# Lag tables of a state-space convolution stored entry by entry, with two products of a complex step in one VectorE instruction

## The chip, the core and the metric

The kernel runs on one core of one Trainium2 chip: TensorE (PE in the profile) multiplies matrices, VectorE (DVE) and ScalarE (ACT) do elementwise work and empty the accumulators (PSUM), SyncE (SP) issues all DMAs, GpSimd (POOL) does a few memsets. The metric is the device time of one execution in microseconds (us), the median of several runs.

## The reference, cut to what matters

Two branches over x (2048 tokens, 512 channels) are mixed by a gate per token.

```python
g = sigmoid((x * gate_w).sum(-1, keepdims=True))
a = attention(x)          # 32 heads of 16, 4 segments of 512 tokens, causal softmax + a memory of earlier segments, then @ wo
dt = exp(log_dt)[:, None]
P = exp((dt * A)[:, :, None] * l)                  # A complex, (512 channels, 128 states); l = 0..2047 rounded to bf16
K = einsum('dn,dnl,dn->dl', C, P, dt * B).real     # convolution kernel, one value per channel and lag
b = irfft(rfft(x) * rfft(K)) + x * Dskip           # causal convolution along the tokens
return g * a + (1 - g) * b
```

Only 640 different lags are left when l is rounded to bf16. The kernel writes each lag as a sum of two exponents, one from a list F_EXP (20 entries) and one from G_EXP (32 entries: 0, 8, ... 248). With z = exp(dt A), K at lag f + g is the real part of a sum over the 128 states of (z to the f) times (C dt B z to the g).

## The kernel before, in words

**Stages.** A preparation computes z and its squares z^2, z^4, ... (ten powers for each half of the channels; the program calls them pw, 512 bf16 values per table of 128 channels: real, real, imaginary twice with a minus sign on one copy, so that a complex product becomes two elementwise products and one sum). Then three things share the engines. Attention works by segment and head group: projections, scores in four banks of PSUM, one exponential of 128x2048 on ScalarE per score tile (line 1068, 80 of them), products with V, norms. The first level of a Fourier transform of x goes to DRAM and back. And `tables(c)` builds, for each quarter c of the channels, the two **lag tables** F (20 entries) and G (32 entries) with the 128 states on the partitions. When all four tables are through, the convolution runs: 32 steps u, each with one product K (five matmuls of 512 columns, line 1273), an elementwise product Y (line 1281), a product V. Sixteen final blocks (line 1307) add the attention's output projection, the inverse transform and the skip term, and scale by the gate. The first matmuls of a final block load weights whose columns lie 16 values (32 bytes) apart.

**A lag table.** Five copies put the first entries in place (tag tabc). Then `cmul` makes n new entries from n old ones by multiplying them with one power: line 1165 multiplies by the first 256 values of the power into the new entries, line 1168 multiplies by the other 256 into a scratch tile t2, line 1172 adds t2 with its halves swapped. Each is one VectorE instruction of 256 n values per partition. A table has 13 such steps: n = 1 three times, n = 2 four times, n = 4 three times, n = 8 three times. That is 39 instructions for a table, 156 in all.

**The layout before.** Channels are stored in pairs: for the real part and then the imaginary part, 64 channel pairs; within a pair all entries, each as two neighbouring channel values. So one new entry (n = 1) is 128 runs of two values (4 bytes), 80 bytes apart in F and 128 bytes in G. The **lag products** (line 1213) take for one channel the 32 entries of G as weights (128x32) and the 20 entries of F as moving columns, each entry 4 bytes behind the one before. Per table there are 256 of these pairs of weight load and matmul, in 8 groups of 32 (four channels at a time in four column groups of the array); the result goes through one copy per half (line 1215) and four small DMAs to a tile KTT, which every K product reads.

**What sets the order.** Nothing is scheduled at run time. ORDER is a list made beforehand: it names every operation by number in one sequence, the engine of each copy that may go to either (a = ACT, v or no letter = DVE), and the buffer. Each engine runs its operations in the order of the list and waits on semaphores for the operations it needs.

Of the kernel before, what the change touches and what calls it, by code (L numbers as in the profile page):

```python
# [98 lines left out]
class Sched:  # L99
# [45 lines left out]
    def ap(self, T, off=0, dims=None, p0=0, np_=128, n=None, dt=None, pstep=1):  # L145
        dt = dt or T.dt
        T = T.tile
        esz = 4 if dt == F32 else 2
        if T.isp:
            h = self.ps32 if dt == F32 else self.ps16  # L150
            base = T.slot * 2048 // esz
        else:
            h = self.sb32 if dt == F32 else self.sb16
# [5 lines left out]
        return bass.AP(v.tensor, v.offset + p0 * st + base + off, [[pstep * st, np_]] + [list(d) for d in dims])  # L159

# [208 lines left out]
0/0 10/0 9/1 23/0/0 24v 15/0 29/0 31/0 38/1 32/2 30/3 33/4 13/2 14/3 27/4/1 39/5 37/6 34 35 40/7 54/0 57/1 6/0 36  # L369
193/0 4/0 41 42 43 44/8 48/0 45/9 46/10 12/4 47 49/11 53/0 50/12 17/0 61/1 59/0 62v/0 51/13 58a/0 60 71/1 52 65/2 11/5  # L370
55/2 56v 73/2 7/0 74v/1 25/3/2 26a 200/5/0/0 201a 250/0/1/1 72 83/3 1247/1 1250/6/0 214/1/0/0 28v 215 75 86v/2 205/0
85/3 173/4 3/0 21/0 66/5 16/0 253/2/0 84 95/0 178/6 20/0 18/0 97/7 98a/3 1226/0 176/1 1/0 251a 96 107/2 63 181/3
1248/7 254a 109/0 1249a 22/0 99 110v/4 202 67 189/0 108 377/0 208/3 190 177/0 252 203/0/1 204a 174/0 196/2 255/0/1/1
191 1251a 119/2 240/0/0 87 79/1 241 120/2 111 209a 122v/5 100 121 123 394/3/1 179/1 256 175 257 133/3 182 88 242
996v/0 395a 131/2 124 132 219/0/1 220 221 146a/6 77/0 998v/0 134v/7 192/0 1003/0 135 143/3 206/3 76 995v 212/0 1002
228/0/2 217 64 994v 1004 145/7 997v 213a 112 1008 1009/1 144 216 1252 229 230 78 1010 210/0 211a 1000/0 223/0/3 224
197/0 198/0 1015/1 147 158v/8 1014 999 136 1016 157/4 207a 235/1 1229/2/1 159 89/2 1001 1012/1 225 222/0 1017 155/3
1230a 1237/3/0 1018/0 1238a 799/0 266/0/1 267 293/2/2/2 226 156 1005 227 231 199/0 268 1011 91/0 1013 236/0/3 167a/9
148 1026 294a 237 588/0 589/3 590 160 168 1020 238 1021/1 232/0 169 90 233 334/2/0/0 335a 1019 1227/3 1228a 234/0
262/0/2 263 1231 264 337/2/2 338a 1022 800/3 239 243 244 1239/0 1240a 245/1 1241 101/0 1029 271/0/3 272 1024/0 273 801  # L380
# [81 lines left out]
def fft_consts():  # L462
# [35 lines left out]
    return W1, M2, N2, G2  # L498


F_EXP = [1, 3, 5, 7, 2, 4, 6, 8, 258, 260, 262, 264, 516, 520, 772, 776, 1032, 1288, 1544, 1800]
G_EXP = [8 * j for j in range(32)]


# [925 lines left out]
```

## Time and profile before

| what | value |
|---|---|
| median of 3 runs | 305.98 us (304.79 to 306.7) |
| the profiled execution | 305.48 us, of which its span is 303.3 us |
| mean granted TensorE clock | 0.958 |
| PE, DVE, ACT busy | 263.6, 264.7, 263.1 us |

The span is the time from the first to the last instruction; some 2.2 us of the execution lie around it. A line number in a row of the profile is a line of the program; most matmuls carry the helper's line 686, and copies out of PSUM the lines 226 (on ACT) and 227 (on DVE). Two successive instructions of DVE or ACT overlap a little, so the time that an instruction takes of its engine is the distance to the next start (the pitch here), not its own length.

### The profile page before, as it was taken

To read this page: it belongs to the slowest core of one execution; us is meant where nothing else is said; L and a number is where in the kernel's file an instruction comes from. 1 tells how busy PE (TensorE), PEld (TensorE's weight loads), DVE (VectorE), ACT (ScalarE), POOL (GpSimd) and SP (SyncE) were. 2 spreads that over 40 slices of the span, in tenths; PEclk is the share of its full clock that TensorE was granted. 3 is DMA by queue.
4 is the path that set the end of the run, shared out by engine and by line. 5 is a ranking of instruction groups with operands and counts; after the bars stand their busy time and mean duration, and the time that the engine had idled before them with its cause. 6 is when DMAs were issued, how large, how long until landed. Compare 5 with 4: busy or idle time off the path is not lost.

```text
span 303.3 us, 9592 instructions
## 1 busy us (share of the span) xinstructions
PE 263.6 (87%) x4078; PEld 150.3 (50%) x4078; DVE 264.7 (87%) x639; ACT 263.1 (87%) x315; POOL 3.2 (1%) x9
## 2 busy tenths in 40 slices
PE   2697698799687888788889999999999999999992
PEld 1442355665344544565446555555545455546551
DVE  2999999999999998999998799999999869957171
ACT  3999999999999899999989998998899999985321
POOL 2000000000000000000000000000000000000000
PEclk9999899789996879999979999999999999999999
DMA  6983722216012331630500516766767756741033
GB/s 150 276 216 90 130 73 71 71 28 185 19 52 53 111 98 40 197 93 17 134 2 18 145 59 197 208 197 180 210 169 212 200 157 187 208 143 46 11 152 126
DMA packets 45002, 37.37 MB, mean 123 GB/s; under 512 B 21408, under 2 KB 40864, under 8 KB 44960
## 3 DMA queue, kind: packets, MB, share of 16 engines
q1 hardware_dynamic: 44960, 36.77, 43.0%
q8 instruction: 32, 0.52, 0.7%
q14 instruction: 10, 0.08, 0.1%
HBM read 18.54 MB, written 6.29 MB: 82 GB/s over the span
## 4 chain that ended last, share of the span: by engine, by line
PE 52%; DVE 22%; ACT 17%; DMA 4%; issue 2%; SPq 1%; ACTq 0%
PE psum L686 51%; ACT sb L1068 9%; DVE sb L1168 5%; DVE sb L1172 5%; ACT sb L226 4%; DVE sb L1165 4%; DMA sb<-in_A_wo_dram 2%; DMA sb<-in_B_log_dt_dram 1%; ACT sb L794 1%; SPq L222 1%; DMA sb<-sb 1%; ACT sb L948 1%; ACT sb L802 1%; DVE sb L227 1%; DVE sb L1122 1%
## 5 line engine op out<-in xcount | busy, mean ns | idle before, releaser
L686 PE MATMUL psum<-sb 128*32 128x20 bf16 (+11 forms) x3990 | 256.4, 232 | 26.0 <-ACT sb L1068 15.0
L686 PEld LDWEIGHTS psum<-sb 128*128 128x128 bf16 (+3 forms) x3990 | 143.6, 97 | 136.6 <-ACT sb L1068 30.0
L1068 ACT ACTIVATE sb<-psum 128x2048 bf16<-128x2048 f32 x80 | 151.4, 1893 | 7.4 <-PE psum L686 6.4
L226 ACT ACTIVATE sb<-psum 128x512 bf16<-128x512 f32 (+2 forms) x152 | 86.1, 615 | 6.8 <-PE psum L686 6.2
L227 DVE CAST sb<-psum 128x512 bf16<-128x512 f32 (+1 forms) x50 | 32.9, 674 | 6.1 <-PE psum L686 5.6
L1165 DVE TENSOR_TENSOR sb<-sb 128x512 bf16<-128x512 bf16 (+3 forms) x52 | 33.9, 660 | 0.1
L1172 DVE TENSOR_TENSOR sb<-sb 128x512 bf16<-128x512 bf16 (+3 forms) x52 | 33.8, 662 | 0.2
L1168 DVE TENSOR_TENSOR sb<-sb 128x512 bf16<-128x512 bf16 (+3 forms) x52 | 33.7, 658 | 0.1
L1080 DVE TENSOR_TENSOR sb<-sb 128x1024 bf16<-128x1024 bf16 (+1 forms) x40 | 22.5, 575 | 1.1 <-ACT sb L1068 0.8
L1281 DVE TENSOR_TENSOR sb<-sb 128x1024 bf16<-128x1024 bf16 x32 | 21.8, 685 | 1.2 <-ACT sb L226 0.8
L229 ACT ACTIVATE sb<-psum,sb 128x512 bf16<-128x512 f32 (+1 forms) x8 | 5.4, 688 | 13.4 <-PE psum L686 13.4
L1043 DVE TENSOR_TENSOR sb<-psum,sb 128x256 bf16<-128x256 f32 x32 | 13.2, 419 | 0.4
L230 DVE TENSOR_SCALAR sb<-psum,sb 128x512 f32<-128x512 f32 (+1 forms) x8 | 6.0, 748 | 8.4 <-PE psum L686 8.3
L794 ACT ACTIVATE sb<-sb 128x512 f32<-128x512 f32 x18 | 11.7, 667 | 0.0
L1040 DVE RECIPROCAL sb<-psum 128x16 f32<-128x16 f32 x32 | 8.0, 250 | 1.7 <-PE psum L686 1.7
L742 PE MATMUL psum<-sb 128*128 128x128 bf16 x24 | 3.1, 309 | 6.8 <-DMA sb<-in_B_A_re_dram 4.1
L1122 DVE TENSOR_TENSOR sb<-psum,sb 128x512 bf16<-128x512 f32 x12 | 8.3, 688 | 0.3
L1338 DVE SCALAR_TENSOR_TENSOR sb<-psum,sb 128x512 bf16<-128x512 f32 x8 | 5.5, 746 | 3.0 <-PE psum L686 3.0
L948 ACT ACTIVATE sb<-psum 128x512 bf16<-128x512 bf16 x12 | 7.7, 638 | 0.5 <-PE psum L945 0.4
L795 DVE TENSOR_TENSOR sb<-sb 128x256 f32<-128x256 f32 x18 | 7.4, 416 | 0.5 <-ACT sb L794 0.5
L999 ACT ACTIVATE sb<-sb 128x512 bf16<-128x512 bf16 x12 | 7.6, 633 | 0.0
L796 DVE SCALAR_TENSOR_TENSOR sb<-sb 128x256 f32<-128x256 f32 x18 | 7.5, 417 | 0.0
(67 smaller groups left out, 105.1 us busy)
## 6 DMA issues: line engine op xcount, KB each, us to landing
sb<-sb SPq DMA_DIRECT2D x64, 128.0 KB, 3.1
sb<-c_DN SPq DMA_DIRECT2D x32, 224.0 KB, 3.1
scr_Z<-sb SPq DMA_DIRECT2D x16, 256.0 KB, 2.4
sb<-scr_Z SPq DMA_DIRECT2D x16, 256.0 KB, 3.5
sb<-in_A_x_dram SPq DMA_DIRECT2D x5, 512.0 KB, 4.6
out_dram<-sb SPq DMA_DIRECT2D x8, 256.0 KB, 2.0
sb<-sb SPq DMA_DIRECT2D x20, 64.0 KB, 2.2
sb<-c_M SPq DMA_DIRECT2D x4, 256.0 KB, 4.4
```

Source lines behind the costliest of these rows:

```text
L226: fa = lambda e: e.activation(dst(), src(), ACT.Copy)
L227: fd = lambda e: e.tensor_copy(dst(), src())
L686: mm = lambda e, o_, l, r_, st, sp, **kw: e.matmul(o_, lhsT=l, rhs=r_, start=st, stop=sp, skip_group_check=True, **kw)
L794: op("ACT", ("As", 512), lambda e, sq=sq, Z=Z: e.activation(ap(sq, n=512), ap(Z, n=512), ACT.Square), r=[Z], w=[sq], key=PW[h] + PWS * k)
L1043: op("DVE", ("V1", 256), lambda e: e.tensor_tensor(ap(o1, gi * 16, [[128, 4], [32, 4], [1, 16]]), ap(T, dims=[[68, 4], [17, 4], [1, 16]]), ...
L1068: o = op("ACT", ("Ax", 2048), lambda e, P=P, pT=pT: e.activation(ap(pT, n=2048), ap(P, n=2048), ACT.Exp, scale=0.25), r=[P], w=[pT])
L1080: op("DVE", ("V2", 128 * nb), lambda e, pT=pT, dims=dims: e.tensor_tensor(ap(pT, dims=dims + [[1, 128]]), ap(pT, dims=dims + [[1, 128]]), ...
L1122: op("DVE", ("V1", 512), lambda e: e.tensor_tensor(ap(o2, 0, [[128, 4], [16, 8], [1, 16]]), ap(P2, 0, [[256, 4], [17, 8], [1, 16]]), ap(R2 ...
L1165: op("DVE", ("V2", 256 * n), lambda e: e.tensor_tensor(run(tile, ne, dst, 1), run(tile, ne, src, sstep), ap(pw, cl * 512, [[2, 128], [0, n ...
L1168: op("DVE", ("V2", 256 * n), lambda e: e.tensor_tensor(run(t2, n, 0, 1), run(tile, ne, src, sstep), ap(pw, cl * 512 + 256, [[2, 128], [0, ...
L1172: op("DVE", ("V2", 256 * n), lambda e: e.tensor_tensor(D_(), D_(), ap(t2, n * 128, [[-n * 128, 2], [2 * n, 64], [1, 2 * n]]), ALU.add), r= ...
L1281: op("DVE", ("V2", 1024), lambda e, Y=Y, XAB=XAB, K3=K3, xo=xo: e.tensor_tensor(ap(Y, dims=[[512, 2], [1, 512]]), ap(XAB, xo, [[512, 2], [ ...
```

## The change

Layout: a table now holds its entries one behind the other, each as 256 neighbouring values (128 real, 128 imaginary). One new entry is one run of 256 values. For the lag products the columns of one channel now lie 256 values (512 bytes) apart, both as weights and as moving columns.

Steps: lines 1165 and 1168 become one instruction of 512 n values: its outer dimension of two goes over the two halves of the power, reads the same old entries twice (step 0) and writes first into the table and then into t2, at the distance between the two tiles. The sum stays one instruction of 256 n values. F_EXP is reordered so that a table needs 12 steps: n = 1 once (G), n = 2 five times, n = 4 three times, n = 8 three times. That is 24 instructions for a table, 96 in all. No DMA is added or removed (207 before and after).

```diff
-F_EXP = [1, 3, 5, 7, 2, 4, 6, 8, 258, 260, 262, 264, 516, 520, 772, 776, 1032, 1288, 1544, 1800]
+F_EXP = [1, 3, 6, 8, 2, 4, 262, 264, 258, 260, 5, 7, 520, 516, 776, 772, 1032, 1288, 1544, 1800]
...
+    def adr(self, T):
+        return (T.pool.addr + T.slot * T.pool.size) // 2
...
-            op("DVE", ("V2", 256 * n), lambda e: e.tensor_tensor(run(tile, ne, dst, 1), run(tile, ne, src, sstep),
-                                                                 ap(pw, cl * 512, [[2, 128], [0, n], [1, 2]]), ALU.mult),
-               r=rd + [pw], w=wr + [tile])
-            op("DVE", ("V2", 256 * n), lambda e: e.tensor_tensor(run(t2, n, 0, 1), run(tile, ne, src, sstep),
-                                                                 ap(pw, cl * 512 + 256, [[2, 128], [0, n], [1, 2]]), ALU.mult),
-               r=rd + [pw], w=[t2])
-            D_ = lambda: ap(tile, 2 * dst, [[ne * 128, 2], [2 * ne, 64], [1, 2 * n]])
+            both = lambda: S.adr(t2) - S.adr(tile) - 256 * dst
+            op("DVE", ("V2", 512 * n), lambda e: e.tensor_tensor(
+                ap(tile, 256 * dst, [[both(), 2], [256, n], [1, 256]]), ap(tile, 256 * src, [[0, 2], [256 * sstep, n], [1, 256]]),
+                ap(pw, cl * 512, [[256, 2], [0, n], [1, 256]]), ALU.mult), r=rd + [pw], w=wr + [tile, t2])
+            D_ = lambda: ap(tile, 256 * dst, [[256, n], [128, 2], [1, 128]])
             op("DVE", ("V2", 256 * n), lambda e: e.tensor_tensor(
-                D_(), D_(), ap(t2, n * 128, [[-n * 128, 2], [2 * n, 64], [1, 2 * n]]), ALU.add), r=[t2], w=wr)
+                D_(), D_(), ap(t2, 128, [[256, n], [-128, 2], [1, 128]]), ALU.add), r=[t2], w=wr)
...
-        fm(1, 0, 1, 1, 1)
+        fm(1, 0, 5, 2, 1)
...
-        fm(2, 0, 1, 2, 2)
+        fm(10, 0, 1, 2, 2)
...
-        fm(6, 4, 1, 1, 2)
...
-        fm(8, 4, 1, 4, 8)
-        fm(12, 5, 2, 4, 9)
+        fm(6, 2, 1, 4, 8)
+        fm(12, 3, 2, 4, 9)
...
-                                i = mm(e, ap(P, sl * NF, n=NF, p0=32 * dq, np_=32), ap(G, (1 - cc) * GPL + (dl // 2) * 2 * NG + dl % 2, [[2, NG]]),
-                                       ap(F, cc * FPL + (dl // 2) * 2 * NF + dl % 2, [[2, NF]]), cc == 0, cc == 1, tile_position=(0, 32 * dq))
+                                i = mm(e, ap(P, sl * NF, n=NF, p0=32 * dq, np_=32), ap(G, (1 - cc) * 128 + dl, [[256, NG]]),
+                                       ap(F, cc * 128 + dl, [[256, NF]]), cc == 0, cc == 1, tile_position=(0, 32 * dq))
```

The ORDER list is replaced as a whole. What it changes can be counted from the two lists. Over the whole program five copies of 512 columns out of PSUM go from ACT to DVE (144 to 139 on ACT, 48 to 53 on DVE), one of 1024 columns goes the same way, two casts of powers (lines 802 and 803) too, and two of the tables' first copies go from DVE to ACT. The sequence of stages stays as it was; the first nine K products come in the same order (u = 3, 2, 0, 1, 10, 4, 7, 5, 8). In front of two of them, the lists hold:

| in front of the K product, in the list | before | after |
|---|---|---|
| first (u = 3): DVE operations | 413 | 363 |
| of these steps of the tables | 156 | 96 |
| the rest of the difference | | 2 casts of powers, 2 copies of 512 and 1 of 1024 out of PSUM, 3 small operations of norms, 1 mask of 512, 2 of the memory's state, 1 of the keys more; 2 first copies of tables fewer |
| first: ACT operations | 199 | 198 (2 copies of 512, 1 of 1024 and 2 casts of powers fewer; 2 first copies of tables, 1 of the gate, 1 of the state more) |
| first: exponentials of 128x2048 among these | 48 | 48 |
| ninth (u = 8): DVE operations | 478 | 420 |
| the rest of the difference, beside the tables | | 1 copy of 1024, 2 casts of powers, 2 sums of 272 of the memory's state more, 2 first copies of tables fewer, copies of 512 the same, small ones one fewer |
| ninth: ACT operations | 227 | 225 (1 exponential of 128x2048, 1 copy of 512, 1 of 1024, 2 casts of powers fewer; 2 first copies and 1 of the gate more) |
| ninth: PE operations | 372 | 371 |

At the end of the list, the load of the output weights (19, 512 KB) still stands on SP behind the load CD30, which waits for the buffer that V25 reads last; between V25 and the first final block the PE's list holds the same products as before, except that V27 and V29 are replaced by V26 and X31 (V is two matmuls of 512 columns, X one).

More of the change, by code (lines that the diff above doesn't have):

```diff
@@ L368 @@
 ORDER = """
[L369 to L378, printed above, removed]
@@ L455 @@
+1624v 1658/5 1659 1619/6 1660 1661/0 1639/1 1625/4 1648 1640 1626/2 1627 1630/1 1631a 1665 1620 1621 1628 1662v 1666
+1667/3 1593/3 1594/4 1606/4 1644 1668a 1653/1 1645/5 1603/2 1595 1604/3 1654 1655 1656 1605v 1632/6 1633 1634 1599/3
+1600 1601 1649 1650 1657a 1612/2 1613/2 1614 1669/5 1670 1641 1671 1672 1607 1675/1 1646a 1676 1602 1673v 1677 1608
+1663 1678/1 1679v 1651a 1652 1615 1674 1680/3 1681 1682 1683 1684v 1685
 """
@@ L1141, in tables @@
         NF, NG = 20, 32
-        FPL, GPL = NF * 128, NG * 128
         fp = {}
```

166 lines of the change are left out of this document (84 added, 82 removed).

## The prediction

> **What bounds the kernel now.** I read the page first, then the busy time by stage, then the chain of work that ended last in order of time, and last the groups by form for the instructions that the change touches.
>
> ```profile
> span 303.3 us, 9592 instructions
> PE 263.6 (87%) x4078; PEld 150.3 (50%) x4078; DVE 264.7 (87%) x639; ACT 263.1 (87%) x315; POOL 3.2 (1%) x9
> PE 52%; DVE 22%; ACT 17%; DMA 4%; issue 2%; SPq 1%; ACTq 0%
> ```
>
> Three engines stand at 87%, so the average names none. The stages do (columns: stretch, its length, busy time of PE, weight loads, DVE, ACT, POOL, granted clock, DMA share, GB/s). I cut them at the first lag products of tables 0 to 3 (about 60, 92, 126 and 160), at the convolution (177) and at the final blocks:
>
> ```profile
> 0.00:60.00 60.00, 43.49 (x609) 24.75 (x611) 53.33 (x147) 53.52 (x75) 1.87 (x7) 0.94 0.53 136
> 60.00:92.00 32.00, 26.59 (x492) 15.67 (x480) 31.61 (x78) 31.15 (x40) 0.66 (x1) 0.95 0.23 67
> 92.00:126.00 34.00, 28.71 (x713) 17.77 (x717) 32.09 (x82) 32.22 (x41) 0.00 (x0) 0.85 0.30 91
> 126.00:160.00 34.00, 28.20 (x516) 17.34 (x513) 33.49 (x78) 31.51 (x38) 0.65 (x1) 0.95 0.29 76
> 160.00:177.00 17.00, 16.18 (x458) 10.21 (x456) 14.25 (x43) 16.22 (x15) 0.00 (x0) 1.00 0.35 97
> 177.00:263.00 86.00, 85.94 (x997) 45.09 (x998) 79.07 (x178) 80.09 (x91) 0.00 (x0) 1.00 0.64 181
> ```
>
> Until 160, DVE and ACT are both full (from 60 to 160 DVE is busy 97.2 of 100 us, ACT 94.9) while PE leaves 16.5 us of those 100 unused. From 177 on it is the other way round: PE is busy 85.94 of 86 us. So there are two phases. The first ends when DVE and ACT have done what the lag products and the K products need; the second lasts as long as PE's queue. The chain (start, length, what) agrees:
>
> ```profile
> 45.83 1.08 DVE sb L1165
> 58.99 1.21 PE psum L686 x115
> 153.71 0.34 DVE sb L1043
> 169.54 3.01 DMA sb<-sb
> 172.64 1.65 PE psum L686 x21
> 178.82 21.11 PE psum L686 x265
> 200.55 62.20 PE psum L686 x689
> 262.79 5.90 DMA sb<-in_A_wo_dram
> 268.83 29.20 PE psum L686 x268
> 298.05 0.75 DVE sb L230
> ```
>
> It runs through table steps on DVE before the first lag products (58.99) and nearly up to 154, through the small DMAs that bring the last lags to KTT (169.54), and from 178.82 through PE to the end. A microsecond saved on DVE before 160 counts if ACT follows; one saved on DVE after 177 counts nothing.
>
> **The change part by part.** First the price of a table step. Here are one kind of step by form (last number before the bar's end: mean ns of one), and starts in the timeline:
>
> ```profile
> L1165 DVE TENSOR_TENSOR sb<-sb 128x2048 bf16<-128x2048 bf16 x12 | 14.5, 1209 | 0.0
> L1165 DVE TENSOR_TENSOR sb<-sb 128x1024 bf16<-128x1024 bf16 x12 | 8.2, 686 | 0.1
> L1165 DVE TENSOR_TENSOR sb<-sb 128x512 bf16<-128x512 bf16 x16 | 6.5, 415 | 0.0
> L1165 DVE TENSOR_TENSOR sb<-sb 128x256 bf16<-128x256 bf16 x12 | 4.9, 410 | 0.0
> ```
>
> ```profile
> 41.77 0.69 DVE L1165 TENSOR_TENSOR sb<-sb 128x1024 bf16<-128x1024 bf16 x1
> 42.38 0.69 DVE L1168 TENSOR_TENSOR sb<-sb 128x1024 bf16<-128x1024 bf16 x1
> 50.65 0.42 DVE L1165 TENSOR_TENSOR sb<-sb 128x512 bf16<-128x512 bf16 x1
> 50.99 0.42 DVE L1168 TENSOR_TENSOR sb<-sb 128x512 bf16<-128x512 bf16 x1
> 52.34 1.22 DVE L1168 TENSOR_TENSOR sb<-sb 128x2048 bf16<-128x2048 bf16 x1
> 53.48 0.42 DVE L1172 TENSOR_TENSOR sb<-sb 128x512 bf16<-128x512 bf16 x1
> 65.24 0.41 DVE L1165 TENSOR_TENSOR sb<-sb 128x256 bf16<-128x256 bf16 x1
> 65.56 0.37 DVE L1168 TENSOR_TENSOR sb<-sb 128x256 bf16<-128x256 bf16 x1
> ```
>
> The pitch (start to next start) is 1.14 us for 2048 values, 0.61 for 1024, 0.34 for 512 and 0.32 for 256. From 512 upwards it is 0.07 fixed plus 0.52 per 1024. At 256 it should be 0.20 and is 0.32: these are the n = 1 steps, whose runs are two values long, and they go at half the rate. Lines 1168 and 1172 have the same forms and counts, so the steps take 3 x (12 x 1.14 + 12 x 0.61 + 16 x 0.34 + 12 x 0.32) = 90.8 us now.
>
> After the change, the double product has 512 n values and the sum 256 n. With 4096 values at 0.07 + 4 x 0.52 = 2.2 (an estimate, by the slope), a table takes 0.34 + 5 x 0.61 + 3 x 1.14 + 3 x 2.2 = 13.4 for the products and 0.20 + 5 x 0.34 + 3 x 0.61 + 3 x 1.14 = 7.2 for the sums. Four tables take 82.2: **8.6 us less on DVE**. Bounds: if the one n = 1 sum per table stays at 0.32, 8.1; if the new shape lost its rate the loss would be large, and that is a rival below. The first copies of a table stay at the same size; I cost their new layout at nothing.
>
> The list then gives work back to DVE and takes it off ACT. A copy of 512 out of PSUM costs 0.61 on DVE or 0.49 on ACT, a cast of powers 0.33 or 0.52:
>
> ```profile
> 12.92 0.61 DVE sb L227
> 26.03 0.49 ACT sb L226
> 27.03 1.77 ACT sb L1068
> 39.52 0.52 ACT sb L802
> 64.59 0.33 DVE sb L803
> ```
>
> ```profile
> L226 ACT ACTIVATE sb<-psum 128x1024 bf16<-128x1024 bf16 x2 | 2.0, 1003 | 0.0
> ```
>
> In front of the first K product, with the counts of the section on the change: DVE -8.6 + 0.7 (casts) + 1.2 (two copies) + 0.6 (copy of 1024 bf16, taken like 512 from float32) + 1.6 (eight small ones at 0.2, an estimate between the fixed 0.07 and L1043's 0.34) - 0.3 (two first copies) = -4.8. ACT: -1.0 (two copies) - 0.9 (copy of 1024) - 1.0 (casts) + 1.2 (four small ones at 0.3, an estimate below the 0.49 of 512 values) = -1.7. In front of the ninth, where PE's list is as long as before: DVE -8.6 + 0.6 + 0.7 + 0.7 (two sums) - 0.3 = -6.9, and ACT, with one exponential of 1.77 fewer, -1.8 - 0.5 - 0.9 - 1.0 + 0.9 = -3.3. Since both engines are full in the first phase and wait for each other, I take the mean of the two reliefs, 3.25 and 5.1, and the middle between the marks: **4.2 us earlier**. The bounds are ACT's smallest relief (1.7) and DVE's largest (6.9, for which ACT would have to use the 5.1 us that it idles between 60 and 160).
>
> Now what speaks against it: the lag products. Half a table of them, 128 pairs, took 1.21 us (the chain's row at 58.99; some of the 128 records are missing). Their columns lie 4 bytes apart now and will lie 512 bytes apart. The nearest row is that of the final blocks, whose first matmuls load columns 32 bytes apart (here three such loads at 273.1), beside all loads of this shape:
>
> ```profile
> L686 PEld LDWEIGHTS psum<-sb 128*128 128x128 bf16 x3 | 0.3, 147 | 0.1
> ```
>
> ```profile
> L686 PEld LDWEIGHTS psum<-sb 128*128 128x128 bf16 x2454 | 125.5, 99 | 94.1 <-issue 20.5 <-ACT sb L226 5.5 <-DVE sb L1043 5.0
> ```
>
> 147 ns for 99, or 48% more. If the whole pair grew so, a half would take 0.6 more; if the four column groups hide it, nothing. I take 0.3 per half: 0.6 for the last table, which lies on the path to KTT, and the other three tables in PE's idle time (16.5 us between 60 and 160). The upper bound is another matter, since 512 bytes is far beyond 32: the n = 1 steps on DVE say half rate for short runs, which is 1.2 more per half and 2.4 on the path.
>
> The Trainium skill (Advanced Engine Details and Errata, SBUF Cachelines) states that SBUF is read in lines of 16 bytes and that full speed needs at least two hits on a line. The half rate of the n = 1 steps agrees with it (410 ns for 256 values, 415 for 512). By this rule each column of a lag product would pay in the new layout; at half rate the sum would be 4.2 - 2.4 - 0.2, a gain of 1.6 us instead of 3.4.
>
> **The rest.** The double product waits for the t2 buffer as line 1168 did, whose last reader is DVE itself: no new wait. It holds DVE up to 1.1 us longer in one piece, 12 times; what comes ready meanwhile (norms, masks, copies for PE) waits half of that on average, 6.4 us if each hit the path, 1.4 at DVE's 22% of the chain; I take 0, because the list was made with that piece in it, and leave 1.4 to the range. SP passes the same DMAs; four per table still follow each other, as in 169.54's row. In the second phase PE's work is unchanged, so it moves as a whole. The load of the output weights took 5.90 us and was just late (268.83); one product V of two matmuls has become an X of one in front of it, 0.2 later. The last copy and store do not change.
>
> **Sum.** 4.2 - 0.6 - 0.2 = 3.4 us less. The profiled execution took 305.48 us (span 303.3), which gives 302.1 (305.48 - 3.4). The median, 305.98, lies 0.5 above that execution; the runs spread over 1.9, so I leave it at **302.1 us**.
>
> **The rivals.**
> - **ACT holds the first phase.** For it: ACT is full too (94.9 of 100), and its relief in front of the first K product is 1.7 only. Against: ACT has idle time that ends when DVE is quicker. The gain is 1.7 - 0.6 - 0.2 = 0.9, less up to 1.4 for the long pieces: 304.6 to 306, say 305.
> - **The lag products become the bound (slower).** Place: the 128x32 loads and 128x20 matmuls. If the four column groups took turns, a half would take four times 1.21, or 3.6 more. The last table puts 7.3 on the path; of the other three, 21.8, I count half, since PE is idle for about a sixth of that phase and scores for ACT queue behind them. 305.5 - 4.2 + 0.2 + 18.2 = 319.7. With d more per half the loss is 2 d + 3 d; it eats the remaining gain of 4.0 at d = 0.8, a half of 2.0 us. A half at double time (d = 1.2) gives 305.5 - 4.0 + 6.0 = 307.5. For it: no row shows a moving operand with a stride at all. Against: the 48% row.
> - **The double product does not run at the quick rate.** The products hold 96256 values; at half rate they cost 0.52 more per 1024, 49 us, and DVE would end the first phase near 210: about 350. Against: line 1168 reads its power with a step of 0 too and runs at full rate.
> - **Full relief.** ACT uses its idle time and the lag products cost nothing: 305.5 - 6.9 = 298.6.
>
> **How the numbers follow.** Forecast (300 to 304) 0.52; ACT holds 0.21; lag products 0.16; slow double product 0.04; full relief 0.07. The measurement can tell about 1% (3.1 us) from no change. Faster by more than 1% means below 302.9: three quarters of the forecast's share (0.39, since 302.1 lies below that bound) and full relief, 0.46. Slower by more than 1%, above 309.0: the lag products from d = 1.5 on (0.13 of the 0.16) and the slow product, 0.17. Within 1%: what is left, 0.37. The range goes from full relief, 298.5, to lag products at double time, 307.5; it leaves out the 0.17 of the slow cases and little below.
>
> **What would show it.** In the changed profile: 96 table steps with 4096 values at about 2.2 us pitch and the steps near 82 us; the 256-value sums at about 285 ns (410 less 0.12); half a table's lag products at 1.5 us; the first K product near 170 instead of 172.64, and PE full from there to the end as before. It would be wrong if a half takes over 2 us, if the first K product comes no earlier although DVE's steps shrank, or if PE shows new idle time after the first K product.

## The result, and the profile after

The changed kernel takes 314.3 us (median of 4 runs, 313.2 to 316.48) against 305.43 us for the kernel before on the same chip (4 runs, 304.79 to 306.7): a ratio of 1.029 with an interval of 1.023 to 1.036. It is slower, by 8.9 us, where a gain of 3.4 was forecast. The profiled execution took 314.6 us.

The page of the changed kernel, its span, its busy times and its chain by engine:

```profile
span 312.8 us, 9530 instructions
PE 275.5 (88%) x4078; PEld 160.4 (51%) x4078; DVE 262.7 (84%) x585; ACT 259.4 (83%) x309; POOL 3.2 (1%) x9
PE 57%; ACT 26%; DVE 6%; DMA 6%; issue 2%; SPq 1%; ACTq 0%
```

PE has the same 4078 matmuls and is busy 11.9 us longer (275.5 for 263.6). DVE's share of the chain fell from 22% to 6%: the engine that the change relieves really left the path, and the time still grew. By stage, cut at the same points as before (first lag products of tables 0 to 3 at 61, 97, 129 and 168, convolution at 185):

```profile
0.00:61.00 61.00, 41.16 (x482) 23.18 (x483) 50.92 (x125) 50.72 (x72) 1.87 (x7) 0.92 0.52 131
61.00:97.00 36.00, 32.40 (x602) 20.00 (x600) 32.41 (x70) 33.63 (x42) 0.65 (x1) 0.85 0.25 75
97.00:129.00 32.00, 28.95 (x594) 18.57 (x598) 29.27 (x66) 30.03 (x38) 0.00 (x0) 0.84 0.30 87
129.00:168.00 39.00, 34.74 (x685) 22.29 (x681) 34.20 (x70) 34.28 (x43) 0.65 (x1) 0.91 0.22 60
168.00:185.00 17.00, 17.00 (x400) 10.90 (x395) 13.32 (x42) 13.23 (x14) 0.00 (x0) 0.90 0.34 92
185.00:274.00 89.00, 87.81 (x1042) 46.70 (x1041) 82.28 (x183) 81.46 (x90) 0.00 (x0) 1.00 0.63 181
```

The picture of the first phase has turned round. DVE and ACT, which were full, have holes in every stage (from 61 to 168 DVE is busy 95.9 of 107 us, ACT 97.9), PE is at 90% of these 107 us, and its granted clock (third column from the right) is 0.84 to 0.91 where it was 0.85 to 0.95. The first elementwise product Y of the convolution (query of its line: instructions by buffer address, first and last start) shows how late the second phase begins; first the kernel before, then the changed one:

```profile
L1281 DVE TENSOR_TENSOR sb<-sb x8: 679/682/693, 178.3 to 198.6; 128x1024 bf16<-128x1024 bf16 x8
```

```profile
L1276 DVE TENSOR_TENSOR sb<-sb x4: 683/688/693, 184.9 to 190.6; 128x1024 bf16<-128x1024 bf16 x4
```

178.3 became 184.9: 6.6 of the 9.5 us that the span grew were lost before the convolution began, and 2.9 behind it. The chain of the changed kernel names the places (start, length, what):

```profile
47.58 0.37 SPq L225
47.99 3.87 DMA sb<-sb
51.89 1.23 DVE sb L1164
97.26 10.86 PE psum L686 x312
128.65 3.91 PE psum L686 x146
135.87 7.84 PE psum L686 x124
167.62 12.01 PE psum L686 x347
206.25 4.21 DMA sb<-c_DN
```

The lag products of tables 1, 2 and 3 (starts 97.26, 128.65, 167.62) begin pieces of the chain, with all that queues behind them on PE. For tables 1 and 3 that is not new. The chain of the kernel before holds, beside table 0's (58.99, shown in the prediction), two pieces with lag products of tables 1 and 3 in them:

```profile
95.71 7.59 PE psum L686 x168
161.77 5.77 PE psum L686 x223
```

In the changed kernel, ahead of table 0's stands a DMA that brings one power (47.99), for which a table step on DVE waits; in the second phase a load of c_DN has come onto the chain. Last, the groups by form that the change touches, the kernel before and then the changed one:

```profile
L686 PE MATMUL psum<-sb 128*32 128x20 bf16 x1024 | 10.4, 179 | 3.6 <-DVE sb L1172 1.9 <-issue 1.6
L686 PEld LDWEIGHTS psum<-sb 128*32 128x32 bf16 x1024 | 9.1, 96 | 6.8 <-issue 4.2 <-DVE sb L1172 2.4
```

```profile
L1164 DVE TENSOR_TENSOR sb<-sb 128x4096 bf16<-128x4096 bf16 x12 | 27.4, 2283 | 0.0
L1168 DVE TENSOR_TENSOR sb<-sb 128x256 bf16<-128x256 bf16 x4 | 1.1, 282 | 0.0
L686 PE MATMUL psum<-sb 128*32 128x20 bf16 x1024 | 19.4, 221 | 1.5 <-ACT sb L229 1.3
L686 PEld LDWEIGHTS psum<-sb 128*32 128x32 bf16 x1024 | 18.2, 169 | 5.5 <-issue 2.7 <-ACT sb L229 1.7 <-DVE sb L1168 1.1
```

The steps on DVE came out as forecast (2283 ns, 282 ns). The lag products did not: the loads take 169 ns for 96, and the 1024 matmuls cover 19.4 us where they covered 10.4. In the timeline a half of 128 products (the first row counts four other matmuls with them, the second one) is:

```profile
97.26 2.87 PE L686 MATMUL psum<-sb 128*32 128x20 bf16 x132 [1.16 <-ACT sb L229]
167.62 2.64 PE L686 MATMUL psum<-sb 128*32 128x20 bf16 x129 [0.18 <-ACT sb L229]
```

Measured start to start, a group of 32 products takes 0.535 us (before: 0.267). A half of four groups takes 2.3 us instead of 1.21: d, the growth of a half, is 1.1, where the prediction put 0.3.

### The profile page after: what moved, and what is told of

The parts are those of the page before. It is cut to its first block, busy times and chain, and to the rows that moved or that the text cites. A ratio compares the mean times of both kernels' runs of the same rounds, so it can differ in the third digit from the quotient of the medians.

```text
span 312.8 us, 9530 instructions
## 1 busy us (share of the span) xinstructions
PE 275.5 (88%) x4078; PEld 160.4 (51%) x4078; DVE 262.7 (84%) x585; ACT 259.4 (83%) x309; POOL 3.2 (1%) x9
## 4 chain that ended last, share of the span: by engine, by line
PE 57%; ACT 26%; DVE 6%; DMA 6%; issue 2%; SPq 1%; ACTq 0%
PE psum L686 57%; ACT sb L1068 14%; ACT sb L229 8%; DMA sb<-in_A_wo_dram 2%; ACT sb L794 1%; DVE sb L1164 1%; DMA sb<-in_B_log_dt_dram 1%; DMA sb<-c_DN 1%; DMA sb<-sb 1%; DVE sb L1168 1%; ACT sb L948 1%; DVE sb L230 1%; SPq L225 1%; ACT sb L999 0%; ACT sb L802 0%
## 5 line engine op out<-in xcount | busy, mean ns | idle before, releaser
L686 PE MATMUL psum<-sb 128*128 128x17 bf16 (+11 forms) x3990 | 269.2, 245 | 24.9 <-ACT sb L1068 14.8
L686 PEld LDWEIGHTS psum<-sb 128*128 128x128 bf16 (+3 forms) x3990 | 153.6, 116 | 137.9 <-ACT sb L1068 31.6
L229 ACT ACTIVATE sb<-psum 128x512 bf16<-128x512 f32 (+2 forms) x146 | 82.4, 616 | 12.9 <-PE psum L686 12.3
L1164 DVE TENSOR_TENSOR sb<-sb 128x1024 bf16<-128x1024 bf16 (+3 forms) x48 | 56.7, 1192 | 1.9 <-DMA sb<-sb 1.6
L230 DVE CAST sb<-psum 128x512 bf16<-128x512 f32 (+1 forms) x55 | 36.7, 678 | 7.6 <-PE psum L686 6.9
L1168 DVE TENSOR_TENSOR sb<-sb 128x512 bf16<-128x512 bf16 (+3 forms) x48 | 31.2, 668 | 0.1
L232 ACT ACTIVATE sb<-psum,sb 128x512 f32<-128x512 f32 (+1 forms) x8 | 5.4, 686 | 8.9 <-PE psum L686 8.8
L794 ACT ACTIVATE sb<-sb 128x512 f32<-128x512 f32 x18 | 12.2, 686 | 0.0
L230 DVE COPY sb<-psum 128x1024 bf16<-128x1024 bf16 x4 | 2.7, 684 | 5.2 <-PE psum L742 5.2
```

What stands on the lines that cost most here:

```text
L229: fa = lambda e: e.activation(dst(), src(), ACT.Copy)
L230: fd = lambda e: e.tensor_copy(dst(), src())
L686: mm = lambda e, o_, l, r_, st, sp, **kw: e.matmul(o_, lhsT=l, rhs=r_, start=st, stop=sp, skip_group_check=True, **kw)
L794: op("ACT", ("As", 512), lambda e, sq=sq, Z=Z: e.activation(ap(sq, n=512), ap(Z, n=512), ACT.Square), r=[Z], w=[sq], key=PW[h] + PWS * k)
L1164: op("DVE", ("V2", 512 * n), lambda e: e.tensor_tensor(ap(tile, 256 * dst, [[both(), 2], [256, n], [1, 256]]), ap(tile, 256 * src, [[0, 2] ...
L1168: op("DVE", ("V2", 256 * n), lambda e: e.tensor_tensor(D_(), D_(), ap(t2, 128, [[256, n], [-128, 2], [1, 128]]), ALU.add), r=[t2], w=wr)
```

## The experiments

**Theory.** The distance of 512 bytes costs PE 1.1 us per half, eight times, and each of them counts, because PE is on the path of the first phase as well. **Rival 1:** the new list is what loses (other engines, the late power). **Rival 2:** ACT, not DVE, held the first phase, so that a relief of DVE could give nothing.

### Distance and list, each alone

The changed kernel with the columns read 4 bytes apart (as before), and the kernel before with its columns read 512 bytes apart (the edit of the first is shown; the second is its reverse):

```diff
-ap(G, (1 - cc) * 128 + dl, [[256, NG]]), ap(F, cc * 128 + dl, [[256, NF]])
+ap(G, (1 - cc) * GPL + (dl // 2) * 2 * NG + dl % 2, [[2, NG]]), ap(F, cc * FPL + (dl // 2) * 2 * NF + dl % 2, [[2, NF]])
```

> The changed kernel with its list and its table steps, but the lag products read columns 4 bytes apart, at the addresses of the old layout. They multiply values that do not belong together, so the lags are not those of the reference. Theory A (the distance of 512 bytes costs everything that was lost: lag products at double time and a TensorE clock that is halved for longer): a group of 32 pairs back from 0.535 to 0.27 us, the time 301 to 303 us. Theory B (the new list is the worse one by itself): the groups are quick and the time stays above 307 us.

Measured: 307.89 us (4 runs), 1.011 of the kernel before (1.005 to 1.016).

> The kernel before, with its list and its table steps, but the lag products read columns 512 bytes apart, at the addresses of the new layout (so the lags are not those of the reference). Theory A: groups at 0.535 us and a loss of 9 to 13 us, 314 to 318 us. Theory B: only the last table lies on the path, 2 to 3 us, 308 us.

Measured: 314.52 us, 1.030 (1.023 to 1.037). With the two kernels themselves this is a table of four:

| median, us | columns 4 bytes apart | columns 512 bytes apart |
|---|---|---|
| list and steps before | 305.1 | 314.5 |
| list and steps after | 307.9 | 314.3 |

The distance costs 9.4 us in the old list and 6.4 in the new. It is the larger cause by far. But with the distance taken away the change is still no gain: list and steps together lose 2.8 us. Where it goes is seen from the first Y to the end of the span (columns as in the table by stage), in the kernel before and then in the one with near columns, whose first Y starts at 176.9:

```profile
178.30:303.30 125.00, 119.15 (x1319) 63.98 (x1317) 98.62 (x213) 97.14 (x110) 0.00 (x0) 0.99 0.54 158
```

```profile
176.90:305.80 128.90, 122.01 (x1346) 65.48 (x1344) 102.69 (x220) 98.08 (x107) 0.00 (x0) 0.99 0.51 155
```

The first Y comes 1.4 us earlier, and behind it 3.9 us are lost: 27 matmuls more stand there (1346 for 1319), which makes PE 2.9 us busier, and PE is idle 1.0 us longer. Three transfers stand on the chain of this kernel that did not stand on it before, the last two behind the first Y:

```profile
48.96 4.24 DMA sb<-sb
198.72 4.47 DMA sb<-c_DN
243.13 4.45 DMA sb<-sb
```

The changed kernel takes 127.9 us from its first Y to the end, the old list with far columns 126.1 (first Y at 188.6). So in these executions the list loses behind the first Y, and the distance ahead of it: 10.3 us in the old list, 8.0 in the new. Which matmuls the new list moved there was not taken apart.

### Operand distance by itself

A small kernel that only streams lag products (512 pairs of each kind, four column groups) with the columns of both operands 2, 4, 8, 16, 32, 128 and 512 bytes apart, and with one operand near and the other far.

> The lag products alone: for each distance between columns 512 pairs of a 128x32 load and a 128x20 matmul in four column groups, with 24 matmuls of 512 columns ahead of each. Nothing of the reference is computed; zeros are stored. Distances in bytes (weights, moving): 2, 4, 8, 16, 32, 128, 512 for both, then 512 and 4, then 4 and 512. If a line of 16 bytes has to be used twice for full speed: 8.4 ns a pair up to 8 bytes and 16.7 from 16 bytes on. If only long distances cost (banks): 8.4 up to 32 or 128 bytes and 16.7 at 512. With one operand far: in between, 32 of 52 columns being weights; if they cost one by one, 13.5 and 11.6 ns.

Groups by form; L472 is 4 bytes, L476 8, L480 16, L492 512, L496 far weights with near moving columns, L500 the reverse:

```profile
L492 PE MATMUL psum<-sb 128*32 128x20 bf16 x512 | 9.3, 221 | 4.0 <-issue 4.0
L480 PE MATMUL psum<-sb 128*32 128x20 bf16 x512 | 8.8, 216 | 4.0 <-issue 4.0
L480 PEld LDWEIGHTS psum<-sb 128*32 128x32 bf16 x512 | 8.3, 160 | 2.7 <-issue 2.7
L496 PE MATMUL psum<-sb 128*32 128x20 bf16 x512 | 8.3, 209 | 4.5 <-issue 4.5
L500 PE MATMUL psum<-sb 128*32 128x20 bf16 x512 | 5.5, 209 | 4.3 <-issue 4.3
L476 PE MATMUL psum<-sb 128*32 128x20 bf16 x512 | 5.1, 184 | 7.2 <-issue 7.2
L472 PE MATMUL psum<-sb 128*32 128x20 bf16 x512 | 4.8, 181 | 7.5 <-issue 7.5
L472 PEld LDWEIGHTS psum<-sb 128*32 128x32 bf16 x512 | 4.4, 98 | 8.2 <-issue 8.2
```

Up to 8 bytes the 512 pairs take 4.8 to 5.1 us, from 16 bytes on 8.8 to 10.7 (9.5 at 32 bytes, 10.7 at 128, 9.3 at 512): the step lies between 8 and 16 bytes, and what follows does not grow with the distance. The Trainium skill (Advanced Engine Details and Errata, SBUF Cachelines) has the rule for it: lines of 16 bytes, full speed only if a line is hit twice. At 8 bytes two bf16 columns share a line, at 16 none do, and the step lies there. Of the two operands the weights are the dear one (8.3 against 5.5).

### The operands in place

The kernel before with only G (the weights), and with only F (the moving columns), read 512 bytes apart:

```diff
-ap(G, (1 - cc) * GPL + (dl // 2) * 2 * NG + dl % 2, [[2, NG]])
+ap(G, (1 - cc) * 128 + dl, [[256, NG]])
```

> The kernel before, with only the G entries (the weights of the lag products) 512 bytes apart; F, the moving operand, stays at 4 bytes. The data of G are misplaced, so K is wrong, the work is the same. In the measurement by itself, far weights alone took 8.3 us of PE per 512 pairs and far moving columns alone 5.5, both near 4.8, both far 9.3. If PE's time at the lag products sets the loss, this costs (8.3 - 4.8)/(9.3 - 4.8) = 0.78 of the 9.4 us of e2, so 312.5 or so (311 to 314), with the clock again halved for some 40 us in the first phase. If the loss hangs on a threshold (the clock gate, or the groups of four at 0.27 us), it may be much less: 307 to 309.

> The kernel before, with only the F entries (the moving operand of the lag products) 512 bytes apart; the weights G stay at 4 bytes. The data of F are misplaced, so K is wrong, the work is the same. If PE's time sets the loss as measured by itself, (5.5 - 4.8)/(9.3 - 4.8) = 0.16 of 9.4 us: 306.6 (305.5 to 307.5). If the moving operand costs as much as the weights in place, 310.

Measured: far weights 310.12 us, 1.013 (1.008 to 1.019); far moving columns 308.37 us, 1.006 (1.002 to 1.009). By the medians both forecasts missed, in opposite directions; by its ratio (307.2) the moving columns came out as forecast. Groups of 32 products took 0.465 and 0.30 us start to start (0.267 near, 0.535 both far), so PE's own time grew by 6.3, 1.0 and 8.6 us over the 32 groups. The time grew by 4.8, 3.0 and 9.4. The weights carry most of it, as by themselves. By the medians the loss isn't one price per microsecond of PE, but the intervals (2.3 to 5.8 us for the weights, 0.7 to 2.9 for the moving columns) are too wide to say so.

### How much a microsecond of lag products counts

Near and far columns with only one of the two products per channel (the edit in part), and near columns with each product issued twice:

```diff
-                        for cc in range(2):
+                        for cc in range(1):
```

> The kernel before, with one lag product for each channel and not two (the second half of each lag is left out): 512 pairs of load and matmul instead of 1024, 4.3 us less for PE. If PE's time at the lag products counts in full, as the loss of e2 (9.4 us for 8.6 us of PE) suggests: 300 to 301 us. If only the last table counts: 304 us.

> Columns 512 bytes apart as in e2, but only one lag product for each channel as in e11 (so the lags are not those of the reference). A group takes 0.27 us, as long as a whole near group. If PE's time is all that the distance costs: 305 us, as before. If slow reads cost more than their time, for instance by a TensorE clock that is halved for longer: 307 to 309 us.

> The kernel before, near columns, with each lag product issued twice into the same accumulator (the lags come out doubled). A group takes 0.53 us, as with columns 512 bytes apart. If the loss is TensorE's time alone: 313 to 315 us, as in e2. If slow reads cool TensorE's clock beyond that: about 310 us, with half clock for some 24 us as before and not for 44 us as in e2.

Measured: near half 302.77 us, 0.992 (0.988 to 0.996); far half 304.38, 0.998 (0.995 to 1.001); twice 336.25, 1.104 (1.098 to 1.110). Taking 4.3 us of lag products out of PE saves 2.4 us in a kernel where the prediction called three of the four tables hidden. The far half is the control for the distance: 64 far products take PE 1.03 us from the first start to the last, as 128 near ones do, and the time is that of the kernel before. So the distance costs what PE's time at the lag products costs, and nothing beyond it that this run can tell (its interval reaches some 1.5 us below the kernel before and 0.3 above). From the far half to all far columns PE gets 8.6 us more and the time 10.1. Doubling does not fit in this row, for a reason that its waits show (engine, line, waited for, us, times, longest), first the kernel before, then the doubled one:

```profile
PE psum L686 <- issue: 1.6, 2, 1.1
```

```profile
PE psum L686 <- issue: 22.9, 24, 3.6
```

"Issue" is time in which PE waited for nothing that the profile shows. A shortage of instructions would look like this, but no run shows what it was. So this run measures these waits more than the lag products, and it decides nothing here.

### Which relief is worth something

The kernel before with the 12-step exponent list alone (expected: DVE 3.7 us less); with the sums over half the pairs (DVE 13.2 less); with 24 exponentials of 512 values cut to 32, the minimum behind each taken of a constant (ACT 8 less); and with both of the last two. The edits of the sums and of one exponential, in part:

```diff
-D_ = lambda: ap(tile, 2 * dst, [[ne * 128, 2], [2 * ne, 64], [1, 2 * n]])
+D_ = lambda: ap(tile, 2 * dst, [[ne * 128, 2], [2 * ne, 32], [1, 2 * n]])
```

```diff
-e.activation(ap(ek, n=512), ap(P, n=512), ACT.Exp)
+e.activation(ap(ek, n=32), ap(P, n=32), ACT.Exp)
```

> The kernel before in its pair layout with one part of the change alone: the new list of exponents, 12 steps for a table and not 13 (two steps of n = 1 become one of n = 2), the list of the order kept with the dropped steps left out. DVE has 12 instructions fewer, 3.7 us less. If DVE and ACT share the first phase: half of it, 303.5 us. If ACT holds it: 305 us as before.

> The kernel before, with the sums of the table steps (line 1172) over 32 of the 64 channel pairs, so that half of each table lacks its second product. DVE has 13.2 us less to do, all of it in the first phase. Theory C (ACT holds the first phase, DVE's relief is lost): 304 to 305 us. Theory D (DVE holds it): 297 to 299 us. Half and half, as the forecast took it: 299 to 300 us.

> The kernel before, with the 24 exponentials of lines 948 and 999 over 32 of 512 columns and the minimum behind each taken of a constant, so that the attention's memory is not that of the reference. ACT has about 8 us less to do, most of it before the convolution. Theory C: 298 to 300 us. Theory D: 304 to 305 us.

> The edits of e5 and e6 together: half of the tables' sums left out on DVE (13.2 us) and short exponentials on ACT (8 us). Theory F (the two engines wait for each other, so only a relief of both counts): 295 to 297 us. Theory G (ACT has slack, DVE and PE hold the first phase in turn): as e5 alone, 300 to 301 us.

| run | relief expected, us | busy by the page (before: DVE 264.7, ACT 263.1) | us | ratio (interval) |
|---|---|---|---|---|
| 12 steps | DVE 3.7 | DVE 264.5 | 304.7 | 0.999 (0.996 to 1.002) |
| half sums | DVE 13.2 | DVE 252.5 | 300.53 | 0.985 (0.981 to 0.990) |
| short exponentials | ACT 8 | ACT 255.2 | 305.16 | 1.000 (0.997 to 1.003) |
| both | DVE 13.2, ACT 8 | DVE 252.1, ACT 253.7 | 300.18 | 0.982 (0.977 to 0.988) |

Rival 2 falls: ACT's relief is worth nothing that can be told, alone or on top of DVE's. DVE's is worth 4.7 us for the 12.2 that it is less busy, 38%. The 12 steps decide nothing about DVE, because the relief hardly arrived: in the pair layout some of the new steps' products are slow, so that the mean of a form rose from 686 to 742 ns, and DVE is only 0.2 us less busy. (Which places of the entries slow them was not taken apart.)

```profile
L1169 DVE TENSOR_TENSOR sb<-sb 128x1024 bf16<-128x1024 bf16 x12 | 8.9, 742 | 0.0
```

From 60 to 160 DVE and ACT were 97% and 95% busy, and neither repays in full what is taken off it. A reading of this, not shown, is that PE, DVE and ACT pass work round a ring there, and that a list that fixes the order keeps part of the gap that an engine wins as waiting.

### List, steps and the late power

The near-column kernel with table 0's power 9 replaced by power 8, which is there earlier (one of the three steps that take it):

```diff
-        fm(12, 3, 2, 4, 9)
+        fm(12, 3, 2, 4, 8 if c == 0 else 9)
```

> The changed kernel with near columns (as e1), and in table 0 the three steps that multiply with the last power (number 9) take number 8 instead, so table 0 is not that of the reference. In e1 the first of these steps waited 1.6 us on DVE for the DMA of power 9, and K0 came 3.5 us late at the first lag products. If this wait is what the new list lost: 305 us against 307.9. If ACT and PE hold that stretch anyway: 307 to 308 us.

Measured: 306.99 us, 1.004 (1.001 to 1.007), 0.9 us less than with the late power by the medians and 1.9 by the ratios: the wait at 48.96 is gone from the chain, and it is at most a part of the list's loss. The two intervals overlap, so its size isn't shown.

The change repaired: its list, channels in fours so that columns lie 8 bytes apart, and the two products of a step as two instructions one behind the other (the edit in part):

```diff
-ap(F, cc * 128 + dl, [[256, NF]])
+ap(F, cc * FPL + (dl // 4) * 4 * NF + dl % 4, [[4, NF]])
```

> The changed kernel's list and its 12 steps, with the layout repaired: channels in fours, so that a lag product's columns lie 8 bytes apart, and the two products of a step as two instructions one behind the other. The output is the reference's. If the columns' distance is what costs and the new list is slightly worse than the old by itself (the experiment with near columns gave 307.9), this gives 307 to 308, 2 per cent under the changed kernel and 1 per cent over the kernel before. If the list's loss came from the misplaced data or from the 4-byte variant, it comes to the 303 of the old list with 12 steps and fours. If the distance is not the cause, it stays at 314.

Measured: 312.64 us, 1.020 (1.013 to 1.028). Nothing of what was expected came: it is well over 308 with near columns. PE's lag products are as short as they should be (group by form), and DVE is back on the chain (shares of the page):

```profile
L686 PE MATMUL psum<-sb 128*32 128x20 bf16 x1024 | 11.3, 183 | 4.2 <-DVE sb L1172 2.2 <-issue 1.9
```

```profile
PE 45%; DVE 37%; DMA 8%; ACT 4%; issue 2%; SPq 2%; ACTq 0%
```

So either the fours or the split instruction cost 4.7 us over the near-column kernel (3.0 by the ratios). The split alone, with near and with far columns:

```diff
-            op("DVE", ("V2", 512 * n), lambda e: e.tensor_tensor(... [[both(), 2], [256, n], [1, 256]] ...
+                e.tensor_tensor(ap(tile, 256 * dst, [[256, n], [1, 256]]), src_(), pw_(0), ALU.mult)
+                return e.tensor_tensor(ap(t2, 0, [[256, n], [1, 256]]), src_(), pw_(256), ALU.mult)
```

> The changed kernel with near lag columns (as in the experiment with 4 bytes, 307.9; K is built from misplaced data as there) and the double product split into two instructions one behind the other. That adds 48 instructions on DVE and by pitch about 3.4 us of DVE in the first phase (2 x 0.34 - 0.61 for n = 1 and 2, 2 x 1.14 - 2.2 for n = 8). If e17's 4.7 us over the near-column kernel come from the split, this gives 311 to 312.6. If they come from the 8-byte runs of the layout in fours, it stays at 308.

> The changed kernel (512-byte columns, the output is the reference's) with only the double product split into two instructions. If what the one instruction saves on DVE counts in this list, 316 to 318 against 314.3. If PE at the lag products alone holds the first phase, 314 to 315.

Measured: near 312.44 us, 1.020 (1.010 to 1.029); far 315.83, 1.037 (1.030 to 1.043). By the medians the split accounts for all of it, 312.44 against 312.64, and the layout in fours costs nothing that can be told. In the new list the double product is worth 4.5 us with near columns by the medians and 2.7 by the ratios, and with far ones 1.5 and 2.2. In both cases the intervals overlap, so its worth there is likely but not shown.

Last, the changed steps in the old order: the list before, without the 12 operations of the dropped step and the 48 second products, with the double product where the second one stood, columns near.

> The steps and tables of the change (12 steps, double product) in the order of the kernel before: its list, with the 12 operations of the dropped step and the 48 separate second products taken out, each double product standing where its second product stood (five steps moved up, since the products of one table keep their order), and the lag columns near, which misplaces the data of K. DVE falls by the 8.6 us of the prediction and no operation changes its engine. If the new list is what lost 2.8 us at near columns, this lands under the kernel before: 8.6 us at the 36 per cent that a relief of 13.2 us was worth gives 302, and with the first 3.7 us worth nothing as in the 12-step experiment 303.3. If the longer piece on DVE costs what the steps save, 305 to 308, as in the new list.

Measured: 305.77 us, 1.000 (0.996 to 1.005). The steps alone gain nothing in the old order, 8.6 us of DVE notwithstanding (by its page DVE is busy 258.8 us for 264.7), and the new list, at 1.011 with the same steps and columns, is the worse list by some 2 to 3 us. Rival 1 holds as the smaller cause.

### A version that beats both

The list before with the 12 steps, and the channels in fours.

```diff
-            run = lambda T, E, e0, st: ap(T, 2 * e0, [[2 * E, 128], [2 * st, n], [1, 2]])
+            run = lambda T, E, e0, st: ap(T, 4 * e0, [[4 * E, 64], [4 * st, n], [1, 4]])
```

> The kernel before with the 12 steps of e3 and channels stored in fours, so that columns of the lag products lie 8 bytes apart and the runs of one entry are 8 bytes long. DVE has 3.7 us less from the steps and 1.4 us from n = 1 at full rate; the lag products cost 0.5 us more by the row of 8 bytes alone. At e5's exchange (4.7 us for 13.2): 303.5 us. At e3's (0.4 for 3.7): 304.7 us.

Measured: 303.09 us (12 runs), 0.993 (0.990 to 0.996). Runs of 8 bytes free DVE of the half rate of its 256-value steps (286 ns for 410), and 8 bytes is still on the cheap side of PE's step; by form:

```profile
L1166 DVE TENSOR_TENSOR sb<-sb 128x256 bf16<-128x256 bf16 x4 | 1.1, 286 | 0.0
L687 PE MATMUL psum<-sb 128*32 128x20 bf16 x1024 | 11.0, 183 | 3.1 <-DVE sb L1173 2.0 <-issue 1.1
```

What differs from the 12 steps alone (0.999) is that here the relief arrives: the steps of 1024 values are back at 683 ns and DVE is busy 260.4 us by the page, 4.3 less than before and 4.1 less than with the 12 steps in pairs. The 2.1 us won are about half of that.

## Why the prediction was wrong, point by point

- **Price of a table step: right.** A double product of 4096 values was put at 2.2 us of DVE. Counted in the traces until the next DVE instruction starts, all steps together take 79.8 us where they took 88.4, which is the 8.6 of the prediction. In the changed kernel the instruction behind a double product starts 2.21 us after it:

```profile
77.49 2.29 DVE L1164 TENSOR_TENSOR sb<-sb 128x4096 bf16<-128x4096 bf16 x1
79.70 0.25 DVE L1040 RECIPROCAL sb<-psum 128x16 f32<-128x16 f32 x1
```

- **"I take 0.3 per half": wrong, the term mis-sized.** A half grew by 1.1. The row of the loads 32 bytes apart, with 147 ns for 99, was the right alarm; the fault was to halve it on the hope that four column groups hide it. The half rate seen on DVE's short runs, kept as the upper bound at 1.2, was nearly it. The Trainium skill's rule of 16-byte lines (Advanced Engine Details and Errata, SBUF Cachelines) pointed the same way. The sum at half rate, a gain of 1.6, stood beside the forecast. But the step is not the same on both engines: on DVE a run of two values went at half the rate (410 ns) and one of four did not (286), while PE was still quick with two columns in 16 bytes.
- **"0.6 for the last table ... the other three tables in PE's idle time": wrong, one of the two steps that failed.** The distance costs 9.4 us in the old list, for 8.6 us of PE, and 6.4 in the new one, 5.8 more than the term. Idle time spread over the phase did not hide them. The chain of before holds lag products of table 0 (58.99), of table 1 (95.71) and of the last (161.77); the rows that the prediction shows of it leave the last two out. Half the near products out saves 2.4 of 4.3 us.
- **"4.2 us earlier": wrong, the other step that failed.** With near columns the change was credited with 4.0 and loses 2.8, a miss of 6.8. The first Y of that kernel comes 1.4 us earlier and not 4.2, and behind it more is lost (next point but one). It took full engines for binding engines: in the order before, 8.6 us less on DVE gave nothing, and 8 us less on ACT gave nothing; half sums gave 4.7 for 12.2, the 12 steps in fours 2.1 for 4.3. And the list gave most of the relief back: by the pages DVE is 2.0 us less busy than before (262.7 for 264.7), and the 3.7 us taken off ACT were taken off the engine whose relief is worth nothing.
- **"ACT holds the first phase": wrong** as a rival, by the runs with less ACT work.
- **"In the second phase PE's work is unchanged, so it moves as a whole": wrong.** From the first Y to the end the span was 125.0 us; it is 127.9 in the changed kernel and 128.9 with near columns, with PE 2.2 and 2.9 us busier there and a load of c_DN on the chain. The old list with far columns takes 126.1, so most of this is the list's.
- **The load of the output weights, 0.2:** nothing in the runs speaks against it; it is below what they can tell.

The sum in place of the forecast: 305.4, plus 0 for the steps, plus 2 to 3 for the list, plus 6.4 for the distance in that list, 314 to 315. It meets the measured 314.3 by its making, since the 6.4 is the changed kernel less the near-column one. The rival "half at double time" had the mechanism of the distance and, counting three tables half, nearly its price in the new list (6.0). It came to 307.5 because it still credited the 4 us.

**What stays open.** Why 8.6 us of DVE are worth nothing in the old order, when half sums and the 12 steps in fours repay a third to a half: five steps had to be moved in the first and none in the others, and its double product holds DVE for 2.2 us in one piece. Why the new list has more of PE's work behind the first Y. And how much the clock (below) adds: no run holds the clock still.

## What to carry to other kernels

Before a layout is turned for one engine, look at every other engine that reads it: here four columns of an operand in 16 bytes became one, and PE's weight loads went from 96 to 169 ns, while with two in 16 bytes they take 117. Price a microsecond on an engine by taking work off it and timing that, not by its busy share, and look on the page whether the relief arrived: of three engines at 87% ACT paid nothing, DVE mostly a third to a half, and PE, with the most idle time in the first phase, more than half. When an order is searched anew together with a change, try the steps in the old order and the old steps in the new one, since the list can lose what the change wins.

## What the runs showed of the hardware

**The clock of TensorE falls although PE is busy.** Windows of 10 us of the kernel before, then of the changed one (columns as in the table by stage):

```profile
60.00:70.00 10.00, 9.38 (x251) 6.07 (x240) 9.61 (x34) 10.00 (x13) 0.00 (x0) 0.85 0.25 70
```

```profile
60.00:70.00 10.00, 9.95 (x290) 6.50 (x290) 6.97 (x25) 8.60 (x12) 0.00 (x0) 0.50 0.34 107
```

PE has work for 9.95 of 10 us, and the clock granted is 0.50 throughout. Summed over the profiled executions (one of each kernel), without the last microseconds, the clock is halved for 23.9 us in the kernel before, 41.0 in the changed one, 10.2 in the same with near columns, 44.4 in the old list with far columns, 30.7 with far weights and 34.1 with far moving columns, and 27.3 with half the far products, whose PE time is that of the near ones. So a longer time at the lag products and a halved clock go together, loosely, and it need not be the distance: with near products doubled it is 41.0 too. With half sums it is 3.4, so that a part of what they gain may be the clock's.

The far lag products themselves are no slower at the halved clock. In the changed kernel a half of 128 takes 2.10 us from the first start to the last at a clock of 0.50 and at 1.00:

```profile
61.30:63.60 2.30, 2.30 (x130) 2.22 (x128) 1.77 (x8) 2.13 (x2) 0.00 (x0) 0.50 0.67 178
167.60:169.80 2.20, 2.18 (x128) 2.20 (x128) 1.63 (x4) 2.17 (x2) 0.00 (x0) 1.00 0.03 7
```

Matmuls of 128 rows and 512 columns do pay: by the trace they start 426 ns apart at 0.50 and 216 at 1.00. But the clock is not most of the loss. An execution of the old list with far columns took 313.08 us at a mean clock of 0.951, and two of the kernel before took 306.16 at 0.950 and 306.34 at 0.952 (on other chips): some 7 of the 9.4 us remain at a like clock. That the rest is the clock's is argued, not shown. The Trainium skill (TensorE: Matmul & The Clock Gate, Part 1) has the clock come back after one busy window of some 3.4 us; by the window above busy time in the records isn't enough for that, and here the measurement decides. In the small kernel the clock falls in the streams of such products at every distance, without order. Here are 8 bytes and 128 (no DVE or ACT work there; the columns are those above without ACT):

```profile
65.80:78.00 12.20, 5.01 (x514) 4.73 (x514) 0.00 (x0) 0.00 (x0) 0.65 0.02 4
123.70:136.80 13.10, 10.56 (x513) 10.27 (x512) 0.00 (x0) 0.00 (x0) 0.78 0.01 4
```

At 2, 4, 16, 32 and 512 bytes it is 0.68, 0.76, 0.73, 0.77 and 0.64. So by itself neither the distance nor PE's busy share (41% and 81% in the two rows) sets the clock.

**A long stream of near lag products waits between its groups.** In the small kernel 128 pairs at 4 bytes take 1.2 us and are followed by 2.5 us of "issue"; at 512 bytes they take 2.3 us and the wait shrinks:

```profile
53.93 1.21 PE L472 MATMUL psum<-sb 128*32 128x20 bf16 x128 [2.54 <-issue]
152.11 2.33 PE L492 MATMUL psum<-sb 128*32 128x20 bf16 x128 [1.68 <-issue]
```

From start to start 128 pairs then take 3.7 us near and 4.0 far, so the long stream hides most of the distance's cost. The profile doesn't show what PE waits for. In the kernel before PE has 1.6 us of such waits in all, with halves of 128 pairs; with the products doubled it has 22.9.
